# First expert slots of a two-layer MoE: another order for the ranks' chain, the hidden layer's low halves and `w2` on VectorE, earlier turning of the next rows, later weight loads

## The chip, the cores and the metric

The kernel runs on one core of a Trainium2 chip. The metric is device time in microseconds (us). The engines are TensorE (PE in the profile; PEld is its weight load), VectorE (DVE), ScalarE (ACT), GpSimd (POOL) and SyncE (SP), which here only issues DMAs. Each engine works through its own instructions in program order; a wait of one instruction holds everything behind it on that engine.

## The reference

Attention without softmax (a decaying state per head), then two mixture-of-experts layers. Each row goes to one of 8 experts, the one with the largest logit.

```
state = gamma * state + k[t] (outer) v[t];  y[t] = scale * q[t] @ state      # 4 x 8 heads, 768 steps, 64 wide
x = y as 3072 rows of 512
layer 1: e = argmax(x @ w_gate + bias[modality]); g = softmax(..)[e]
         x[row] = g * (relu(x[row] @ w1[e]) @ w2[e])                         # w1[e] 512x1024, w2[e] 1024x512
layer 2: e = argmax(x @ w_gate); g = softmax(..)[e]; o = sigmoid(x @ w_output_gate)[e]
         out[row] = g * o * (relu(x[row] @ w1[e]) @ w2[e])
```

## The kernel before

The attention is a loop of 24 units (line 772, `i` from 0 to 23). Its results are scattered to `x1d` in DRAM, each row at the place of its expert. Then each layer runs over slots of 256 rows, one expert each; which expert a slot has is known only on the chip. A slot fetches its rows into `xqb` (`xqf` in layer 1's first slot), turns them with DVE transposes into `xTb`, splits them into `xh` (ACT) and `xl` (DVE), multiplies by `w1` into `hT` (mm1, 96 matmuls of 256 columns), takes the ReLU as `hh` (ACT, line 960) and `hl` (DVE, line 961), multiplies by `w2` into `po` (mm2, 48 matmuls of 512 columns), and scales the result into `ob` (`done`, DVE, lines 1014 and 1017), which GpSimd scatters. Every product is made in three passes of reduced-precision numbers, high by high, high by low, low by high. So a loaded weight `raw` is split into a high half (`w1h`, `w2h`, ACT) and a low half (`w1l`, `w2l`, DVE, lines 514 and 521; one instruction of `w2l` covers a quarter of `w2`).

The first slot of each layer (`first`, line 1285; `first2` for layer 2) also has the end of the routing in it. The last rows of the layer before are transposed on PE (line 1051), their logits made (`lgm`, `lgs`), an expert chosen (`choose`, lines 185 to 212), ranks counted on PE (lines 218 and 220), and then DVE works out places: `total` (line 226 on), `place`, `weigh`, and `rp.blocks()`, which ends with line 368. This is called the ranks' chain here. Only then can the last rows be scattered, and the rows of the second slot be fetched (`s1.fetch`: half of them on SP's queue, half on ACT's). `rp.slots` (lines 378 to 420) makes the table of all slots.

What stands where in a slot is written by hand: `run` (line 1124) calls `at(f)` ahead of every `f` of mm1 (f = 0 to 7, 12 matmuls each, in the groups 0 to 3, 4 and 5, 6 and 7), and ahead of each eighth of mm2 (8 + j). `FIRST_AT` names the positions of transposes, `lgm`, `lgs`, count and total, place (the chain), scatter, choose, the step between the two transposes, and decide. `FIRST_W2` says at which position each quarter of `w2` is split, "h" on ACT, "l" on DVE. In first slots mm2 goes through its eighths in the order 0, 4, 1, 5, 2, 6, 3, 7; an eighth is six matmuls, and the first four eighths use quarters 0 and 1 of `w2`. Within them come four of `hh` by `w2h`, two of `hl` 0 by `w2h` (twice, once for each half of the rows), then two of `hl` 1, two by `w2l` 0, two by `w2l` 1. At j = 7, behind `done(0)`, the second slot's rows are turned (`Slot.turn`: the DVE transpose and `xh`).

SP's queue takes its DMAs in program order: at the end of attention the loads of q, k and v for the coming units, the first slot's weights, and the first slot's rows.

Of the kernel before, what the change touches and what calls it, by code (L numbers as in the profile page):

```python
# [424 lines left out]
def retention_moe_moe_kernel(ctx: ExitStack, tc: tile.TileContext, q, k, v, mod, mb, wg, wg2, w1, w2, cst_d, out):  # L425
    nc = tc.nc
# [195 lines left out]
    with ExitStack() as actx:  # L622
# [149 lines left out]
        for i in range(n):  # L772
# [57 lines left out]
            if i == i0 + 1:  # L830
                e0 = nc.values_load(rp1.star[0:1, 0:1], engines=[ENG.SP], min_val=0, max_val=E - 1, skip_runtime_bounds_check_because=why)
            if i0 < i <= i0 + 2:
                load(raw1, w1, e0, ks=(2 * (i - i0 - 1), 2 * (i - i0 - 1) + 1))
            if i0 + 2 < i <= i0 + 4:
                load(raw2, w2, e0, ks=(2 * (i - i0 - 3), 2 * (i - i0 - 3) + 1))
            if i == n - 4:
                fetch_rows(x1d, first_row(rp1), 2, xqf, xmf, after=scattered[-4:] + blanks)
        g1, ids = group1(n - 2, n, misc)
        ids()


    with ExitStack() as mctx:
# [30 lines left out]
        class Slot:  # L873
# [84 lines left out]

            def relu(self, b):
                nc.scalar.activation(hh[b], hT[b], AF.Relu)  # L960
                nc.vector.scalar_tensor_tensor(hl[b], in0=hT[b], scalar=0.0, in1=hh[b], op0=ALU.max, op1=ALU.subtract)  # L961

            def mm1(self, fs, at):
# [5 lines left out]
                for i, (m, f, k) in enumerate(todo):  # L969
                    if i % (3 * KD) == 0:  # L970
                        at(fs[i // (3 * KD)])
                    a, b = ((w1h, xh), (w1h, xl), (w1l, xh))[m]
                    nc.tensor.matmul(hT[f // 2][:, (f % 2) * 2 * P:(f % 2 + 1) * 2 * P], lhsT=a[k][:, f * P:(f + 1) * P], rhs=b[:, k, :],  # L973
                                     start=(m == 0 and k == 0 and f % 2 == 0), stop=(m == 2 and k == KD - 1), skip_group_check=True)
# [149 lines left out]
            def run(self, steps=(), nxt=()):  # L1124
# [3 lines left out]
                if not first:  # L1128
# [3 lines left out]
                    else:  # L1132
                        self.split2((0, 1))

                def group(f):
                    at(f)
                    if f == 5:
                        self.prepare()
                    if first:
                        for ks, parts in FIRST_W2[self.li - 1].get(f, ()):  # L1140
                            split2(ks, parts)

                for fs in ((0, 1, 2, 3), (4, 5), (6, 7)):
                    self.mm1(fs, group)
                    for f in fs[1::2]:
                        self.relu(f // 2)
                        if two and f % 4 == 3:
# [5 lines left out]
                for j, i in enumerate((0, 4, 1, 5, 2, 6, 3, 7) if first else range(8)):  # L1153
                    if first or j != 1:
                        group(8 + j)
                    if first and j == 5:
                        self.regs()
                        self.load(raw1, w1)
                        self.load(raw2, w2)
                    if first and j == 6:  # L1160
                        self.split1(0)
                    if j == (7 if first else 1):
                        if not first:
                            self.split1(0, "h")
                        self.coming(nxt, Slot.turn)
                        if not first:
                            group(9)
# [26 lines left out]
            def run_small(self, steps=(), nxt=()):  # L1194
# [21 lines left out]
                for j in range(4):  # L1216
# [29 lines left out]

        BIG_AT, SMALL_AT, FIRST_AT = (4, 7, 8, 15, 16, 16, 9, 1, 3), (1, 2, 4, 8, 8, 8, 5, 0, 2), (3, 4, 5, 6, 6, 8, 5, 0, 3)
        FIRST_W2 = [{3: [((0,), "hl")], 4: [((1,), "hl")], 6: [((2, 3), "h")], 8: [((2, 3), "l")]},
                    {f: [((f - 5,), "hl")] for f in range(5, 9)}]

# [34 lines left out]
        def first(li, steps, g, a, scatter):  # L1285
# [5 lines left out]
            def go(k):  # L1291
                if not rest:
                    rest.append(turns(g["place"](), g["weigh"](), rp.blocks()))
                for _ in zip(range(k), rest[0]):
                    pass
            s.run(steps + [(a, [lambda: go(100)]), (a + 1, [scatter]), (a + 2, [lambda: s1.fetch(after=before(), halves=(1,)), rp.slots]),
                           (max(9, a + 3), [lambda: s1.fetch(after=before(), halves=(0,), queue=nc.scalar)])], [s1])

# [11 lines left out]
        def first2(pend):  # L1310
            g, steps = pend.route(FIRST_AT, banks=[xT, hT[3]])
            run(rp2.order())
            first(2, steps[:7], g, FIRST_AT[4], pend.scatter)
# [83 lines left out]
```

## Time and profile before

| | |
|---|---|
| three runs | 792.72, 795.04 (median), 797.77 us |
| the profiled execution | 793.22 us, of which 791.4 us are its span |
| PE busy | 769.9 us, 97% of the span |
| DVE, ACT, POOL busy | 439.1, 282.4, 179.5 us |
| mean granted clock of PE | 0.999 |

The first slot of layer 1 runs on PE from 131 to 156 us, that of layer 2 from 462 to 489 us. Times of instructions are counted from the start of the span. A row of the timeline has the start and the length of a run of like instructions, and, in brackets, the idle time of the engine just before it with what ended that. Matmuls overlap, so the steps between the starts of rows tell what one costs.

### The profile page before, as it was taken

To read this page: it belongs to the slowest core of one execution; us is meant where nothing else is said; L and a number is where in the kernel's file an instruction comes from. 1 tells how busy PE (TensorE), PEld (TensorE's weight loads), DVE (VectorE), ACT (ScalarE), POOL (GpSimd) and SP (SyncE) were. 2 spreads that over 40 slices of the span, in tenths; PEclk is the share of its full clock that TensorE was granted. 3 is DMA by queue.
4 is the path that set the end of the run, shared out by engine and by line. 5 is a ranking of instruction groups with operands and counts; after the bars stand their busy time and mean duration, and the time that the engine had idled before them with its cause. 6 is when DMAs were issued, how large, how long until landed. Compare 5 with 4: busy or idle time off the path is not lost. (4 is left out here: it accounts for less than half of the span.)

```text
span 791.4 us, 18969 instructions
## 1 busy us (share of the span) xinstructions
PE 769.9 (97%) x6123; PEld 670.2 (85%) x6123; DVE 439.1 (55%) x1151; ACT 282.4 (36%) x507; POOL 179.5 (23%) x285
## 2 busy tenths in 40 slices
PE   8999999999999999999999988999999999999996
PEld 7888888788888978988899777888889888899785
DVE  4655488724344438334445887244656486473872
ACT  2444455312212234121212542124353563533641
POOL 4456653301110111110011112011302122011121
PEclk9999999999999999999999999999999999999999
DMA  9989899582211116221132343512716377271621
GB/s 190 184 192 216 219 285 298 186 282 57 56 42 29 42 44 234 66 56 41 45 82 70 137 148 108 190 53 69 254 38 236 80 247 249 54 239 46 223 71 53
DMA packets 137408, 107.06 MB, mean 135 GB/s; under 512 B 70269, under 2 KB 113405, under 8 KB 137216
## 3 DMA queue, kind: packets, MB, share of 16 engines
q1 hardware_dynamic: 125712, 85.15, 40.0%
q0 software_dynamic: 6400, 18.98, 6.5%
q10 hardware_dynamic: 5104, 0.75, 0.7%
q8 instruction: 74, 1.21, 0.7%
q14 instruction: 118, 0.97, 0.4%
HBM read 167.64 MB, written 25.83 MB: 244 GB/s over the span
## 5 line engine op out<-in xcount | busy, mean ns | idle before, releaser
L960 ACT ACTIVATE hh<-hT 128x512 fp32r<-128x512 f32 x96 | 57.3, 597 | 251.0 <-PE hT L973 251.0
L961 DVE SCALAR_TENSOR_TENSOR hl<-hT,hh 128x512 fp32r<-128x512 f32 x96 | 65.0, 687 | 131.5 <-ACT hh L960 113.4
L995 PE MATMUL po<-w2h,hl 128*128 128x512 f32 x400 | 113.9, 399 | 1.4 <-DVE hl L961 0.8
L995 PE MATMUL po<-w2l,hh 128*128 128x512 f32 x400 | 110.3, 396 | 1.8 <-DVE ob L1238 1.3
L995 PE MATMUL po<-w2h,hh 128*128 128x512 f32 x400 | 110.9, 399 | 0.0
L973 PE MATMUL hT<-xl,w1h 128*128 128x256 f32 x768 | 107.8, 282 | 0.0
L973 PE MATMUL hT<-xh,w1h 128*128 128x256 f32 x768 | 103.9, 282 | 3.7 <-ACT xh L555 3.5
L973 PEld LDWEIGHTS hT<-xh,w1h 128*128 128x128 f32 x768 | 96.2, 188 | 8.0 <-ACT xh L555 5.3
L973 PE MATMUL hT<-xh,w1l 128*128 128x256 f32 x768 | 102.0, 280 | 0.0
L973 PEld LDWEIGHTS hT<-xl,w1h 128*128 128x128 f32 x768 | 96.5, 188 | 4.5 <-issue 4.5
L973 PEld LDWEIGHTS hT<-xh,w1l 128*128 128x128 f32 x768 | 95.0, 188 | 0.0
L995 PEld LDWEIGHTS po<-w2l,hh 128*128 128x128 f32 x400 | 74.8, 188 | 21.1 <-DVE ob L1238 1.7
L995 PEld LDWEIGHTS po<-w2h,hl 128*128 128x128 f32 x400 | 73.6, 188 | 19.0 <-DVE hl L961 1.5
L995 PEld LDWEIGHTS po<-w2h,hh 128*128 128x128 f32 x400 | 73.1, 188 | 16.7 <-ACTq L1034 1.0
L475 POOL DMA_INDIRECT x2d<-ob,r_idx x28 | 30.3, 1081 | 246.1 <-DVE ob L265 134.3
L1030 POOL DMA_INDIRECT out_dram<-ob,to x28 | 37.1, 1325 | 176.5 <-DVE ob L1017 108.0
L555 ACT ACTIVATE xh<-xTb 128x512 fp32r<-128x512 f32 x58 | 33.4, 623 | 89.3 <-DVE xTb L550 49.3
L521 DVE TENSOR_TENSOR w2l<-raw,w2h 128x1024 fp32r<-128x1024 f32 x44 | 52.1, 1221 | 8.6 <-ACT w2h L519 3.2
L514 DVE TENSOR_TENSOR w1l<-raw,w1h 128x512 fp32r<-128x512 f32 x88 | 54.9, 687 | 0.5 <-ACT w1h L512 0.5
L512 ACT ACTIVATE w1h<-raw 128x512 fp32r<-128x512 f32 (+1 forms) x84 | 48.0, 639 | 1.7 <-ACTq L1038 1.0
L550 DVE STREAM_TRANSPOSE xTb<-xqb 128x1024 f32<-128x1024 f32 x29 | 36.0, 1243 | 22.5 <-DMA xmb<-x1d 10.6
L557 DVE TENSOR_TENSOR xl<-xTb,xh 128x512 fp32r<-128x512 f32 x58 | 37.5, 687 | 13.0 <-ACT xh L555 13.0
(217 smaller groups left out, 971.6 us busy)
## 6 DMA issues: line engine op xcount, KB each, us to landing
raw<-in_w_dram SPq DMA_DIRECT2D x248, 512.0 KB
xqb<-x2d SPq DMA_DIRECT2D x124, 64.0 KB
xqb<-x1d SPq DMA_DIRECT2D x108, 64.0 KB
nq<-in_q_dram SPq DMA_DIRECT2D x48, 128.0 KB
nk<-in_k_dram SPq DMA_DIRECT2D x24, 256.0 KB
nv<-in_v_dram SPq DMA_DIRECT2D x24, 256.0 KB
x1d<-zrow SPq DMA_DIRECT2D x4, 516.0 KB
x2d<-zrow SPq DMA_DIRECT2D x4, 516.0 KB
```

The costliest lines, as they stand in the source:

```text
L475: return nc.gpsimd.indirect_dma_start(out=dst, out_offset=bass.IndirectOffsetOnAxis(ap=rp.idx[:, t:t + 1], axis=0), in_=row, in_offset=Non ...
L512: nc.scalar.activation(w1h[i][:, cols], raw1[i][:, cols], AF.Copy)
L514: los[i].tensor_tensor(w1l[i][:, cols], raw1[i][:, cols], w1h[i][:, cols], op=ALU.subtract)
L521: nc.vector.tensor_tensor(w2l[i], raw2[i], w2h[i], op=ALU.subtract)
L550: nc.vector.transpose(xT[:, ks].rearrange("p k (a i) -> p a k i", i=32), xq.rearrange("p a (k i) -> p a k i", k=KD)[:, :, ks])
L555: nc.scalar.activation(hi[:, k:k + 2, :], xT[:, k:k + 2, :], AF.Copy)
L557: nc.vector.tensor_tensor(lo[:, k:k + 2, :], xT[:, k:k + 2, :], hi[:, k:k + 2, :], op=ALU.subtract)
L960: nc.scalar.activation(hh[b], hT[b], AF.Relu)
L961: nc.vector.scalar_tensor_tensor(hl[b], in0=hT[b], scalar=0.0, in1=hh[b], op0=ALU.max, op1=ALU.subtract)
L973: nc.tensor.matmul(hT[f // 2][:, (f % 2) * 2 * P:(f % 2 + 1) * 2 * P], lhsT=a[k][:, f * P:(f + 1) * P], rhs=b[:, k, :], start=(m == 0 and ...
L995: nc.tensor.matmul(po[h], lhsT=x[b][:, o:o + P], rhs=w[f // 2][:, f % 2, :], start=(m == 0 and f == 0), stop=(m == 2 and f == KF - 1))
L1030: nc.gpsimd.indirect_dma_start(out=out, out_offset=bass.IndirectOffsetOnAxis(ap=to[:, t:t + 1], axis=0), in_=o[:, :DM], in_offset=None, bo ...
```

## The change

- At the end of attention, the second half of `w1` is loaded at `i = n - 4`, behind the last q, k and v (before: one unit sooner), and `w2` at the next two units, behind the rows of the first slot `xqf` (before: half of it ahead of them).
- `relu` can put `hl` off. In first slots `hl` 0, 1 and 2 come at position 6, in `group`, behind `at(6)`.
- `mm1` calls `at` at every half position too.
- `FIRST_AT` has other positions: in layer 2 the transposes stand after 30 matmuls of mm1 (before 36), the logits at 3 and 4, and choose, count, total and the chain between 5 and 5.5; the scatter at 6, fetch and slots' table at 7.
- `FIRST_W2`: layer 1's quarter 0 is split one position sooner on ACT, and the low half of quarter 1 comes at 6 (before 4). In layer 2 the low halves of the quarters come at 7, 8, 9, 9 (before 5, 6, 7, 8).
- The second slot's rows are turned at j = 6, ahead of the split of the next `w1` and of `done(0)`.
- `rp2.order()` moves from the start of layer 2's first slot to behind `choose`.

```diff
@@ attention's loop
-            if i0 < i <= i0 + 2:
-                load(raw1, w1, e0, ks=(2 * (i - i0 - 1), 2 * (i - i0 - 1) + 1))
-            if i0 + 2 < i <= i0 + 4:
-                load(raw2, w2, e0, ks=(2 * (i - i0 - 3), 2 * (i - i0 - 3) + 1))
+            if i in (i0 + 1, n - 4):
+                load(raw1, w1, e0, ks=(0, 1) if i == i0 + 1 else (2, 3))
             if i == n - 4:
                 fetch_rows(x1d, first_row(rp1), 2, xqf, xmf, after=scattered[-4:] + blanks)
+            if n - 4 < i < n - 1:
+                load(raw2, w2, e0, ks=(0, 1) if i == n - 3 else (2, 3))
@@ relu
+            def relu(self, b, later=None):
                 nc.scalar.activation(hh[b], hT[b], AF.Relu)
-                nc.vector.scalar_tensor_tensor(hl[b], in0=hT[b], scalar=0.0, in1=hh[b], op0=ALU.max, op1=ALU.subtract)
+                def low():
+                    nc.vector.scalar_tensor_tensor(hl[b], in0=hT[b], scalar=0.0, in1=hh[b], op0=ALU.max, op1=ALU.subtract)
+                if later is None:
+                    low()
+                else:
+                    later.append(low)
@@ mm1
-                    if i % (3 * KD) == 0:
-                        at(fs[i // (3 * KD)])
+                    if i % 6 == 0:
+                        at(fs[i // (3 * KD)] + i % (3 * KD) / (3 * KD))
@@ run
                     if first:
+                        if f == 6:
+                            for low in later:
+                                low()
                         for ks, parts in FIRST_W2[self.li - 1].get(f, ()):
                             split2(ks, parts)
-                        self.relu(f // 2)
+                        self.relu(f // 2, later if first and f < 6 else None)
                     if first and j == 6:
+                        self.coming(nxt, Slot.turn)
                         self.split1(0)
                     if j == (7 if first else 1):
                         if not first:
                             self.split1(0, "h")
-                        self.coming(nxt, Slot.turn)
-                        if not first:
+                            self.coming(nxt, Slot.turn)
                             group(9)
@@ tables
-FIRST_AT = (3, 4, 5, 6, 6, 8, 5, 0, 3)
-        FIRST_W2 = [{3: [((0,), "hl")], 4: [((1,), "hl")], 6: [((2, 3), "h")], 8: [((2, 3), "l")]},
-                    {f: [((f - 5,), "hl")] for f in range(5, 9)}]
+FIRST_AT = (2.5, 3, 4, 5.5, 5.5, 7, 4, 0, 3)
+        FIRST_W2 = [{2: [((0,), "h")], 3: [((0,), "l")], 4: [((1,), "h")], 6: [((2, 3), "h"), ((1,), "l")], 8: [((2, 3), "l")]},
+                    {5: [((0,), "h")], 6: [((1,), "h")], 7: [((2,), "h"), ((0,), "l")], 8: [((3,), "h"), ((1,), "l")], 9: [((2, 3), "l")]}]
@@ first
-            s.run(steps + [(a, [lambda: go(100)]), (a + 1, [scatter]), (a + 2, [lambda: s1.fetch(after=before(), halves=(1,)), rp.slots]),
-                           (max(9, a + 3), [lambda: s1.fetch(after=before(), halves=(0,), queue=nc.scalar)])], [s1])
+            s.run(steps + [(a, [lambda: go(100)]), (6, [scatter]), (7, [lambda: s1.fetch(after=before(), halves=(1,)), rp.slots]),
+                           (9, [lambda: s1.fetch(after=before(), halves=(0,), queue=nc.scalar)])], [s1])
@@ first2
-            run(rp2.order())
+            steps[4][1].append(lambda: run(rp2.order()))
```

How the change stands in the engines' programs, at three places. The first is VectorE in layer 1's first slot, from the choice (line 209) to the total (line 226), before:

```order
L209 TENSOR_TENSOR r_oh<-rq_643,rm_0_646 128x16
L521 TENSOR_TENSOR w2l_104<-raw_88,w2h_100 128x1024
L961 SCALAR_TENSOR_TENSOR hl<-hT_116,hh 128x512
L961 SCALAR_TENSOR_TENSOR hl<-hT_117,hh 128x512
L521 TENSOR_TENSOR w2l_105<-raw_89,w2h_101 128x1024
L226 TENSOR_TENSOR rR_730<-misc,r_base 128x24
```

In the change one quarter of `w2l` is left there, and the two `hl` and the next quarter come behind the chain's last instruction (line 368), ahead of the slots' table (line 378 on):

```order
L368 TENSOR_SCALAR r_meta<-sfo_2434 128x1
L963 SCALAR_TENSOR_TENSOR hl<-hT_116,hh 128x512
L963 SCALAR_TENSOR_TENSOR hl<-hT_117,hh 128x512
L963 SCALAR_TENSOR_TENSOR hl<-hT_118,hh 128x512
L521 TENSOR_TENSOR w2l_105<-raw_89,w2h_101 128x1024
L378 TENSOR_TENSOR sm_0_2422<-sm_0_2421,cst 128x24
```

So two `hl` and one `w2l` have moved past the chain. The second place is VectorE in layer 2's first slot, behind the chain's end, before (`w2l_104`, quarter 0, stands ahead of the chain there; `w2l_107` is quarter 3):

```order
L368 TENSOR_SCALAR r_meta<-sfo_2437 128x1
L521 TENSOR_TENSOR w2l_105<-raw_89,w2h_101 128x1024
L521 TENSOR_TENSOR w2l_106<-raw_90,w2h_102 128x1024
L961 SCALAR_TENSOR_TENSOR hl<-hT_119,hh 128x512
L378 TENSOR_TENSOR sm_0_2425<-sm_0_2424,cst 128x24
```

In the change three `hl` follow line 368, then the slots' table, and behind its last instruction (line 413) stand all four quarters of `w2l`, `hl` 3 and the turn of the next rows (line 550):

```order
L413 CAST r_meta<-sld_2504 128x1
L521 TENSOR_TENSOR w2l_104<-raw_88,w2h_100 128x1024
L963 SCALAR_TENSOR_TENSOR hl<-hT_119,hh 128x512
L521 TENSOR_TENSOR w2l_105<-raw_89,w2h_101 128x1024
L521 TENSOR_TENSOR w2l_106<-raw_90,w2h_102 128x1024
L521 TENSOR_TENSOR w2l_107<-raw_91,w2h_103 128x1024
L891 TENSOR_LOAD r_meta
L550 STREAM_TRANSPOSE xTb<-xqb 128x8x4x32
```

So every quarter of `w2l` has moved behind the slots' table. The third place is TensorE in the first group of layer 2's mm1, where the last rows of layer 1 are transposed for their logits, before:

```order
L973 MATMUL hT_116<-xh,w1l_99 128x256
L1051 MATMUL xT<-ident,ob_2286 128x128 x4
L1051 MATMUL hT_119<-ident,ob_2286 128x128 x4
L973 MATMUL hT_116<-xh,w1l_96 128x256
L973 MATMUL hT_116<-xh,w1l_97 128x256
```

And in the change, with the logits (`misc<-oT,wgp`) six matmuls of mm1 behind them:

```order
L980 MATMUL hT_117<-xl,w1h_93 128x256
L1058 MATMUL xT<-ident,ob_2286 128x128 x4
L1058 MATMUL hT_119<-ident,ob_2286 128x128 x4
L980 MATMUL hT_117<-xl,w1h_94 128x256
L980 MATMUL hT_117<-xl,w1h_95 128x256
L980 MATMUL hT_116<-xh,w1l_96 128x256
L980 MATMUL hT_116<-xh,w1l_97 128x256
L980 MATMUL hT_116<-xh,w1l_98 128x256
L980 MATMUL hT_116<-xh,w1l_99 128x256
L1064 MATMUL misc<-oT,wgp_75 32x256 x4
```

The two sets of transposes have moved ahead of six matmuls of mm1, and the logits are six matmuls nearer to them.

## Rows read from the trace of the kernel before

**Rows 1.** The page's first part: busy time, share of the span, instructions.
```profile
PE 769.9 (97%) x6123; PEld 670.2 (85%) x6123; DVE 439.1 (55%) x1151; ACT 282.4 (36%) x507; POOL 179.5 (23%) x285
```

**Rows 2.** All waits of PE, 95 to 165 us: total, times, longest (us).
```profile
PE hT L973 <- ACT xh L555: 1.6, 2, 1.3
PE hT L667 <- DVE P L689: 0.7, 1, 0.7
```

**Rows 3.** Timeline of PE, layer 1's first slots: start, length, instruction, [idle before <- releaser].
```profile
139.78 0.18 PE L218 MATMUL misc<-r_oh,cb 128*128 128x16 bf16 x1
...
144.19 1.09 PE L995 MATMUL po<-w2h,hh 128*128 128x512 f32 x4
145.12 0.63 PE L995 MATMUL po<-w2h,hl 128*128 128x512 f32 x2
...
156.87 1.38 PE L973 MATMUL hT<-xh,w1h 128*128 128x256 f32 x7 [1.31 <-ACT xh L555]
...
181.13 0.17 PE L218 MATMUL misc<-r_oh,cb 128*128 128x16 bf16 x1 [0.59 <-DVE r_oh L212]
```

**Rows 4.** Timeline of DVE, layer 1's first slot.
```profile
140.21 1.28 DVE L961 SCALAR_TENSOR_TENSOR hl<-hT,hh 128x512 fp32r<-128x512 f32 x2
141.41 1.22 DVE L521 TENSOR_TENSOR w2l<-raw,w2h 128x1024 fp32r<-128x1024 f32 x1
142.54 0.17 DVE L226 TENSOR_TENSOR rR<-misc,r_base 128x24 f32<-128x24 f32 x1
...
146.07 0.15 DVE L368 TENSOR_SCALAR r_meta<-sfo 128x1 int32<-128x1 int32 x1
...
154.86 1.24 DVE L550 STREAM_TRANSPOSE xTb<-xqb 128x1024 f32<-128x1024 f32 x1
```

**Rows 5.** Timeline of ACT, end of layer 1's first slot.
```profile
156.19 1.15 ACT L555 ACTIVATE xh<-xTb 128x512 fp32r<-128x512 f32 x2 [11.21 <-DVE xTb L550]
```

**Rows 6.** Timeline of PE, layer 2's first slot.
```profile
467.26 0.66 PE L1051 MATMUL xT<-ident,ob 128*128 128x128 f32 x4 [0.94 <-DVE w1l L514]
...
477.33 0.86 PE L995 MATMUL po<-w2h,hh 128*128 128x512 f32 x3
...
481.57 0.73 PE L995 MATMUL po<-w2l,hh 128*128 128x512 f32 x2 [0.34 <-DVE w2l L521]
...
491.19 2.02 PE L973 MATMUL hT<-xh,w1h 128*128 128x256 f32 x15 [1.87 <-ACT xh L555]
```

**Rows 7.** Timeline of DVE, layer 2's first slot.
```profile
476.48 0.17 DVE L226 TENSOR_TENSOR rR<-misc,r_base 128x24 f32<-128x24 f32 x1
...
480.19 0.15 DVE L368 TENSOR_SCALAR r_meta<-sfo 128x1 int32<-128x1 int32 x1
480.29 2.36 DVE L521 TENSOR_TENSOR w2l<-raw,w2h 128x1024 fp32r<-128x1024 f32 x2
...
483.17 0.18 DVE L378 TENSOR_TENSOR sm<-sm,cst 128x24 f32<-128x24 f32 x1
...
484.97 0.14 DVE L413 CAST r_meta<-sld 128x1 int32<-128x1 f32 x1
```

**Rows 8.** Timeline of SP's DMA queue, end of attention.
```profile
120.85 1.88 SPq L538 DMA_DIRECT2D xqf<-x1d  x4
...
129.55 3.50 SPq L461 DMA_DIRECT2D x1d<-zrow  x4
```

**Rows 9.** Busy time in two stretches: engine busy (count), granted clock, DMA share, GB/s.
```profile
120.00:140.00 20.00, 19.59 (x265) 17.43 (x262) 16.21 (x59) 10.84 (x22) 8.68 (x13) 1.00 1.04 313
...
460.00:480.00 20.00, 17.54 (x136) 15.67 (x137) 17.67 (x76) 9.72 (x17) 2.82 (x3) 1.00 0.43 140
```

**Rows 10.** Timeline of ACT, end of layer 2's first slot.
```profile
490.21 1.15 ACT L555 ACTIVATE xh<-xTb 128x512 fp32r<-128x512 f32 x2 [11.13 <-DVE xTb L550]
```

**Rows 11.** Timeline of PE around 446 us, another slot's start.
```profile
445.98 1.16 PE L981 MATMUL hT<-w1h,xh 128*128 128x512 f32 x4 [0.92 <-issue]
```

**Rows 12.** Timeline of DVE, layer 2's second slot.
```profile
503.65 1.29 DVE L961 SCALAR_TENSOR_TENSOR hl<-hT,hh 128x512 fp32r<-128x512 f32 x2 [10.50 <-ACT hh L960]
```

More of the change, by code (lines that the diff above doesn't have):

```diff
@@ L957, in load @@
                 load(raw, w[(self.li - 1) * E:], self.ld[1], cond=self.ld[0], ks=ks)
-            def relu(self, b):
+            def relu(self, b, later=None):
                 nc.scalar.activation(hh[b], hT[b], AF.Relu)
-                nc.vector.scalar_tensor_tensor(hl[b], in0=hT[b], scalar=0.0, in1=hh[b], op0=ALU.max, op1=ALU.subtract)
+                def low():
[4 more added lines that the diff above has]
+                    later.append(low)
             def mm1(self, fs, at):
@@ L1133, in run @@
                         self.split2((0, 1))
+                later = []
                 def group(f):
@@ L1245, in run_small @@
                 at(8)
-        BIG_AT, SMALL_AT, FIRST_AT = (4, 7, 8, 15, 16, 16, 9, 1, 3), (1, 2, 4, 8, 8, 8, 5, 0, 2), (3, 4, 5, 6, 6, 8, 5, 0, 3)
-        FIRST_W2 = [{3: [((0,), "hl")], 4: [((1,), "hl")], 6: [((2, 3), "h")], 8: [((2, 3), "l")]},
-                    {f: [((f - 5,), "hl")] for f in range(5, 9)}]
+        BIG_AT, SMALL_AT, FIRST_AT = (4, 7, 8, 15, 16, 16, 9, 1, 3), (1, 2, 4, 8, 8, 8, 5, 0, 2), (2.5, 3, 4, 5.5, 5.5, 7, 4, 0, 3)
+        FIRST_W2 = [{2: [((0,), "h")], 3: [((0,), "l")], 4: [((1,), "h")], 6: [((2, 3), "h"), ((1,), "l")], 8: [((2, 3), "l")]},
+                    {5: [((0,), "h")], 6: [((1,), "h")], 7: [((2,), "h"), ((0,), "l")], 8: [((3,), "h"), ((1,), "l")], 9: [((2, 3), "l")]}]
         def step(li, i, pend=None):
```

## The prediction

> **What bounds the kernel now.** I read the page first. TensorE (PE) is busy 97% of the span [rows 1], so the 791.4 us can only shrink by the 21 us in which PE stands idle, and a change that moves other engines' work is worth what it takes out of those gaps or puts into them. Next I read PE's waits around the end of attention. From 95 to 165 us there are three: two for ScalarE's `xh` and one for the decay `P`; none is for a q, k or v tile or for a weight [rows 2]. Then I read PE's timeline in the first slot of layer 1: its second product starts at 144.19, and the next slot begins with a wait of 1.31 us for `xh`; later, 0.59 us goes by before the counts of the next slot's routing [rows 3]. VectorE's (DVE's) timeline tells why the rows come late. The ranks' chain (from the total, line 226, to the slots' order, line 368) begins at 142.54, after two low halves `hl` and two of `w2l`; the rows of the next slot, asked for behind it, are turned only after `done(0)`, at 154.86 [rows 4]. `xh` follows at 156.19 [rows 5]. In layer 2's first slot the same pieces lie otherwise: PE waits for the transposes, once for `w2l` (0.34), and 1.87 at the end [rows 6]; DVE has its chain from 476.48 to 480.34, then two `w2l`, then `hl` 3, then the slots' table [rows 7].
>
> **Loads at the end of attention.** The edit changes when 2 MB of weights are asked for, not how many. As no wait there is for q, k or v, asking for weights later takes nothing from PE: I cost it at 0. What covers the later arrival is time: the last parts of `w2` are first split some 12 us after they can be asked for. If that cover is gone, the row fetch is what suffers, since it must land before `xh` and PE's start at 131.17. It was issued at 120.85 and had landed by 129.55, when the zero fill that waits for it went out [rows 8]. Two more half-megabyte loads now stand close behind it. At the 313 GB/s of that stretch [rows 9], 1.05 MB take 3.35 us, so 0 to +3.35 us; I take 0, since they are issued behind the fetch, not ahead of it.
>
> **Layer 1's first slot.** Two `hl` and one `w2l` leave the place ahead of the chain: 1.28 + 1.22 = 2.50 us [rows 4]. The total would then begin at 140.04; the counts that it reads are issued by PE at 139.78 [rows 3], in the same place as before, so nothing new holds it. The chain takes 146.22 - 142.54 = 3.68 us and ends near 143.7. Behind it `hl` 0, 1, 2 take 0.6 each, to 145.5, then `w2l` 1 to 146.7. PE's first use of `hl` 0 is at 145.12 [rows 3]; a 512-column matmul takes 0.93/4 = 0.233 us there. In the code `hl` 1 comes 12 matmuls into the second product (147.0), `w2l` 0 after 14 (147.5) and `w2l` 1 after 16 (147.9). All are ready, by 0.8 us at the least. The scatter, the row fetch and the slots' table move up by about 2.5 us. The rows had been there for a turn at 154.86 without a wait, so they are there by 152.4 now, and the turn stands ahead of `done(0)`. `xh`'s first half ends 1.33 + 0.6 us after the turn starts, at 154.4. The second product ends at 156.87 - 1.31 = 155.56: the wait goes, **-1.31**. The turn puts 1.24 us on DVE ahead of `done(0)`, which nobody on PE waits for there. The 0.59 us of the next slot hangs on rows fetched later in the same queue; earlier requests may remove all or none of it, so I take **-0.3**, with 0 and -0.59 as the bounds. That also covers the loads that follow.
>
> **Layer 2's first slot.** The transposes stand six mm1 matmuls sooner, but in both kernels they wait until 467.26 for results that DVE reaches at its own time [rows 6]. Six matmuls of 256 columns (half of 0.233 each) are then still to do: +0.70. Behind them 60 mm1 matmuls (7.0 us) and the routing's small ones (about 1.0) filled 8.76 us up to 477.33, so some 0.7 us of short waits for the logits and the choice are there to be saved by asking sooner. I take +0.45 (0 to +0.9), and the second product starts at 477.8. The counts now stand 30 mm1 matmuls ahead of that, at about 474.3, so the chain starts about 474.4 and, 3.86 us long [rows 7], ends at 478.3. `hl` 0 is ready at 478.95, while PE wants it 0.93 us into the product, 478.73: +0.2. With `hl` 1 and 2 behind it DVE is free at 480.2. Here the edited table puts `w2l` 0 behind the slots' table, which takes 485.11 - 483.17 = 1.94 us [rows 7]: to 482.1. `w2l` 0 (1.18) is ready at 483.3. PE wants it 14 matmuls in, at 481.3: **+2.0**. Two matmuls later PE wants `w2l` 1, which stands behind `hl` 3: 483.3 + 0.6 + 1.2 = 485.1, against 483.8: **+1.3**. `w2l` 2 and 3 are done at 487.5 and wanted after 490. The old wait of 0.34 goes. Together 0.45 + 0.2 + 2.0 + 1.3 - 0.34 = **+3.6** on PE's second product; the bounds are +2 (chain half done sooner) and +4.5.
>
> **The gap behind it.** The 1.87 us is put down to `xh`. In layer 1 the product began 0.68 us after `xh`'s first instruction started (156.87 and 156.19); here it took 0.98 (491.19 and 490.21) [rows 3, 5, 6, 10]. `xh` was ready 0.3 us before PE began, so something of PE's own ended last. PE also stood for 0.92 us at 445.98, at a jump to another piece of code, with nothing waited for [rows 11]. The page of the Trainium skill "Runtime: NRT & Kernel Launch", section "Instruction fetch mechanics", says that a taken branch to a page of code outside the window breaks the sequential fetch, and the engine stands until the code has come; by that rule the gap follows PE's own branch and earlier rows can't remove it. No row here names what PE does in it. With rows that are now about 2 us earlier and a product that ends 3.6 later, `xh` is certainly early; if it alone set the gap, up to 1.57 us would go, and if PE's own step sets it, nothing goes. The offset of 0.3 us is nearer to the second: **0** (from -1.87). It could also grow: DVE stood 10.50 us ahead of the first `hl` of the next slot, at 503.65, while the next weights were in flight [rows 12]; if PE's step falls into that stretch and takes twice as long, that is +1.9.
>
> **Sum.** -1.31 - 0.3 + 3.6 = +2.0 us. The profiled execution took 793.22, which lies 1.8 below the median of the three runs (795.04); on it the sum gives 795.2, on the median 797.0. I forecast the middle, 796.0.
>
> **Rivals.**
> *The gap goes with the rows.* If `xh` alone sets the 1.87 us: 796.0 - 1.6 = 794.4. For it speaks the label of the wait; against it the 0.3 us. Chance 0.2.
> *Layer 1 gives nothing.* If the row fetch is not asked for sooner, because the landing of the scattered rows holds it, the 1.6 us stay: 797.6. The earlier total speaks against it. Chance 0.1.
> *The table does not stall PE.* If in layer 2 the slots' table is shorter or waits elsewhere and `w2l` arrives in time, +3.6 falls to +0.5 and the time to 792.9. Against it stand the measured 1.94 and 1.18 us. Chance 0.1.
> *The row fetch is slowed by the loads behind it*: +3.35, so 799.4. Chance 0.06.
> *Slower: PE's clock falls.* Two waits of 2.0 and 1.3 us, two matmuls apart, are new. If PE drops to 1.2 GHz after them, the 32 matmuls that are left of the 48 take 32 x 0.233 = 7.5 us more: 803.5, slower by over 1%. It decides only if the drop lasts the whole rest. The granted clock stayed at 1.00, that is 2.4 GHz, in the stretch with 2.46 us of idle time [rows 9]. The Trainium skill, "TensorE: Matmul & The Clock Gate", Part 1, says that the clock follows recent activity and idleness lowers it; this trace shows no drop at gaps as long. Chance 0.04.
>
> **Chances and range.** My forecast has 0.5. A change under 1% (8 us) is about what a measurement of this kernel can't tell from none. All cases but the clock's lie inside 1%: faster 0.02, same 0.93, slower 0.05. The range goes from 791.5 (no stall and the gap gone, on a fast base) to 799.5 (the slowed fetch); the three runs before alone span 5 us.
>
> **What would show it.** In the new trace: no wait for `xh` at the start of layer 1's second slot, with the turn ahead of `done(0)`; DVE's total near 140 there. In layer 2: the slots' table ahead of the first `w2l`, and two waits of PE for `w2l` of about 2.0 and 1.3 us near 481 and 484. The start of the next slot shows whether the gap is still 1.9 us with `xh` done well before. I would be wrong if PE shows no `w2l` wait there, if attention's end shows a new wait for `xTf` or `xqf`, or if the granted clock falls.

## The result and the profile after

| kernel | median us (range, runs) | ratio to the kernel before on the same chip, 95% interval |
|---|---|---|
| before | 795.09 (792.72 to 797.77, 6) | |
| the change | 802.33 (799.59 to 803.99, 6) | 1.0087 [1.0071, 1.0103] |
| the change on a second chip | 798.76 (794.43 to 802.32, 10) | 1.0037 [1.0011, 1.0063] |

The change made the kernel slower, by 7.2 us on the first chip and 3.9 on the second: under 1%, but clear of the noise on both. 796.0 was forecast, 791.5 to 799.5 as the range; the first median lies above it, the second inside. The profiled execution took 802.49 us, its span is 800.6 (before 793.22 and 791.4), and its mean granted clock is 0.988 (before 0.999). The granted clock is that of PE as a share of 2.4 GHz: 0.50 is 1.2 GHz, and a value between is read here as a stretch with some of each. The page of the change, PE's line and the granted clock in 40 slices, shows where to look: before, the clock had nines throughout [rows 1 has PE's line of before].

```profile
PE 775.6 (97%) x6123; PEld 675.2 (84%) x6123; DVE 440.6 (55%) x1151; ACT 282.8 (35%) x507; POOL 182.3 (23%) x285
...
PEclk9999999999999999999999997899999999999999
```

PE is busy for 5.7 us more with the same number of matmuls: they took longer. The slices with 7 and 8 lie from 480 to 520 us, in layer 2's first and second slot. PE's timeline of the change, layer 1's second slot and layer 2's first (start, length, instruction, idle time before it with its releaser):

```profile
157.51 0.75 PE L980 MATMUL hT<-xh,w1h 128*128 128x256 f32 x5
...
466.61 0.66 PE L1058 MATMUL xT<-ident,ob 128*128 128x128 f32 x4 [1.65 <-DVE w1l L514]
...
478.63 1.10 PE L1002 MATMUL po<-w2h,hh 128*128 128x512 f32 x4
...
483.91 0.73 PE L1002 MATMUL po<-w2l,hh 128*128 128x512 f32 x2 [1.57 <-DVE w2l L521]
485.64 1.22 PE L1002 MATMUL po<-w2l,hh 128*128 128x512 f32 x2 [1.00 <-DVE w2l L521]
...
487.52 1.91 PE L1002 MATMUL po<-w2l,hh 128*128 128x512 f32 x4
489.22 1.91 PE L1002 MATMUL po<-w2h,hh 128*128 128x512 f32 x4
...
499.36 3.77 PE L980 MATMUL hT<-xh,w1h 128*128 128x256 f32 x16 [3.19 <-issue]
502.94 3.20 PE L980 MATMUL hT<-xl,w1h 128*128 128x256 f32 x16
```

Layer 1's second slot starts without the wait that stood there [rows 3]. In layer 2 the wait ahead of the transposes has grown from 0.94 to 1.65, two waits for `w2l` (1.57 and 1.00) stand where one of 0.34 was, and the gap ahead of the second slot is 3.19 instead of 1.87 [rows 6]. Behind the waits, four 512-column matmuls take 489.22 - 487.52 = 1.70 us, where they had taken 0.93 [rows 3], and behind the gap sixteen of 256 columns take 502.94 - 499.36 = 3.58. The stretches of the change by window (busy time of PE, PEld, DVE, ACT, POOL; then the granted clock, DMA share, GB/s) say why. The kernel before has 1.00 in each of them.

```profile
460.00:470.00 10.00, 7.58 (x57) 6.33 (x57) 8.58 (x27) 2.87 (x6) 0.57 (x1) 0.90 0.63 216
470.00:480.00 10.00, 9.97 (x80) 8.92 (x73) 6.75 (x49) 6.04 (x9) 3.20 (x4) 0.93 0.14 50
480.00:485.00 5.00, 3.08 (x12) 1.84 (x11) 4.93 (x23) 0.37 (x1) 2.22 (x5) 1.00 0.38 87
485.00:490.00 5.00, 4.36 (x10) 3.47 (x11) 4.01 (x4) 0.89 (x2) 0.00 (x0) 0.50 0.70 211
490.00:495.00 5.00, 5.00 (x19) 3.94 (x18) 0.19 (x1) 0.27 (x1) 0.00 (x0) 0.82 0.95 352
...
500.00:505.00 5.00, 5.00 (x25) 5.00 (x25) 0.00 (x0) 0.00 (x0) 0.97 (x1) 0.50 0.16 60
```

The granted clock is 0.50 (1.2 GHz) from 485 to 490 and from 500 to 505, and below 1.00 around 470. Each time PE had stood idle just before: 1.65 us ahead of the transposes, 1.57 and 1.00 for `w2l`, 3.19 at the slot's end.

Between PE's milestones (the start of the first matmul of each stage in the timeline) the two profiled executions divide so:

| stage, us | before | change | difference |
|---|---|---|---|
| start to layer 2's first mm1 | 461.83 | 461.18 | -0.65 |
| layer 2's first slot, mm1 | 15.50 | 17.45 | +1.95 |
| its second product and the gap | 13.86 | 20.73 | +6.87 |
| second slot's mm1 | 11.30 | 14.07 | +2.77 |
| second slot's second product | 12.71 | 11.20 | -1.51 |
| from there to the last matmul | 269.13 | 268.92 | -0.21 |

Together +9.22. Of the third line, 2.57 - 0.34 = 2.23 are the `w2l` waits, 3.19 - 1.87 = 1.32 the gap, and 0.2 a short wait for `hl` 0 (the first four matmuls take 479.75 - 478.63 = 1.12 instead of 0.93); the 3.1 that are left are matmuls at the lower clock. The fourth line is all clock (16 matmuls in 3.58 us instead of 1.9). Of the second, an execution of the change whose clock stayed at 1.00 there needs 16.05 us (experiment 5), so 0.55 are its own and 1.4 the clock's. That makes about 7.3 us of clock, and 1.9 us net of everything else.

This is one pair of executions, and both are far out. The profile of before, at 0.999, shows less of the low clock than most of its executions: 31 of them on the second chip have 0.993 to 0.998, 0.9965 on the mean. In the change's profile on the second chip the four lines of layer 2 come to +6.45 us instead of +10.08, and by the same division 3.2 of these are the clock's.

VectorE's timeline of the change shows both parts at work. In layer 1 the total begins at 142.16, the turn stands ahead of `done(0)` (line 1021), and DVE then waits 1.22 us for PE to finish that half's product:

```profile
142.16 0.18 DVE L226 TENSOR_TENSOR rR<-misc,r_base 128x24 f32<-128x24 f32 x1 [0.45 <-PE misc L220]
...
145.71 0.15 DVE L368 TENSOR_SCALAR r_meta<-sfo 128x1 int32<-128x1 int32 x1
...
153.85 1.24 DVE L550 STREAM_TRANSPOSE xTb<-xqb 128x1024 f32<-128x1024 f32 x1
156.31 0.75 DVE L1021 TENSOR_SCALAR ob<-po,xmf 128x512 f32<-128x512 f32 x1 [1.22 <-PE po L1002]
```

In layer 2 the first `w2l` comes only behind the slots' table, at 482.64:

```profile
478.94 0.15 DVE L368 TENSOR_SCALAR r_meta<-sfo 128x1 int32<-128x1 int32 x1
479.01 1.88 DVE L963 SCALAR_TENSOR_TENSOR hl<-hT,hh 128x512 fp32r<-128x512 f32 x3
480.80 0.17 DVE L378 TENSOR_TENSOR sm<-sm,cst 128x24 f32<-128x24 f32 x1
...
482.58 0.14 DVE L413 CAST r_meta<-sld 128x1 int32<-128x1 f32 x1
482.64 1.21 DVE L521 TENSOR_TENSOR w2l<-raw,w2h 128x1024 fp32r<-128x1024 f32 x1
483.77 0.68 DVE L963 SCALAR_TENSOR_TENSOR hl<-hT,hh 128x512 fp32r<-128x512 f32 x1
484.37 3.49 DVE L521 TENSOR_TENSOR w2l<-raw,w2h 128x1024 fp32r<-128x1024 f32 x3
```

The next rows' `xh` on ScalarE, and the next expert's weights on SP's queue, in the change:

```profile
489.11 1.15 ACT L555 ACTIVATE xh<-xTb 128x512 fp32r<-128x512 f32 x2 [8.74 <-DVEq L1041]
```

```profile
485.77 5.71 SPq L506 DMA_DIRECT2D raw<-in_w_dram  x8
```

`xh` is done at 490.3, 9 us ahead of the slot that needs it. The gap of 3.19 has nothing to do with the rows.

### The profile page after: what moved, and what is told of

Its sections match the earlier page's. It is cut to its first block, busy times and chain, and to the rows that moved or that the text cites. A ratio compares the mean times of both kernels' runs of the same rounds, so it can differ in the third digit from the quotient of the medians.

```text
span 800.6 us, 18964 instructions
## 1 busy us (share of the span) xinstructions
PE 775.6 (97%) x6123; PEld 675.2 (84%) x6123; DVE 440.6 (55%) x1151; ACT 282.8 (35%) x507; POOL 182.3 (23%) x285
## 5 line engine op out<-in xcount | busy, mean ns | idle before, releaser
L1037 POOL DMA_INDIRECT out_dram<-ob,to x28 | 40.5, 1447 | 189.6 <-DVE ob L1024 113.0
L519 ACT ACTIVATE w2h<-raw 128x1024 fp32r<-128x1024 f32 x44 | 44.4, 1049 | 0.7 <-PE po L1002 0.6
```

Of the source, the lines that this page charges most:

```text
L519: nc.scalar.activation(w2h[i], raw2[i], AF.Copy)
L1037: nc.gpsimd.indirect_dma_start(out=out, out_offset=bass.IndirectOffsetOnAxis(ap=to[:, t:t + 1], axis=0), in_=o[:, :DM], in_offset=None, bo ...
```

## The experiments

Theory A is that PE's new waits in layer 2's first slot let the clock fall and that the clock is the larger part of the loss; theory B that the waits cost their own length only. Theory J is on the gap: it is PE's own step to the next piece of code, lengthened by the weights in flight. All ratios are to the kernel before on the same chip.

**1. The slots' table behind the first `w2l`.**

```diff
-7: [((2,), "h"), ((0,), "l")], 8: [((3,), "h"), ((1,), "l")]
+7: [((2,), "h"), ((0, 1), "l")], 8: [((3,), "h")]
-(7, [lambda: s1.fetch(after=before(), halves=(1,)), rp.slots])
+(7, [lambda: s1.fetch(after=before(), halves=(1,))]), (7 if li == 1 else 8, [rp.slots])
```

> The change with one thing else: in layer 2's first slot the low halves of w2's quarters 0 and 1 stand ahead of the slots' table on DVE, the table behind them. Theory A (the two waits for w2l let PE's clock fall, and the clock is the larger part of the loss): the waits fall from 2.57 us to about 0.4, the stretch from 485 to 492 us runs at a granted clock of 1.00, and the kernel takes 5 to 6 us less than the change (about 797). Theory B (the waits cost their own length, the clock falls for another reason): 2.2 us less (about 800), with the clock still at 0.5 behind the second product's first part.

795.64 us, 1.0008 [0.9993, 1.0022]. Waits and clock of this kernel, PE's timeline and the window:

```profile
482.51 0.73 PE L1002 MATMUL po<-w2l,hh 128*128 128x512 f32 x2 [0.39 <-DVE w2l L521]
...
494.73 3.51 PE L980 MATMUL hT<-xh,w1h 128*128 128x256 f32 x16 [4.49 <-issue]
```

```profile
480.00:490.00 10.00, 9.61 (x42) 7.22 (x40) 9.36 (x27) 1.15 (x2) 1.98 (x4) 1.00 0.53 149
```

The wait fell to 0.39 and the clock stayed at 1.00 through the second product. By the ratios the change is 0.9 or 0.4% above before, and this kernel 0.1%: 6.3 us less than the change by its first result, 2.3 by its second. On this chip experiment 4, the change but for its loads, took 798.02: 2.4 us more, close to the 2.2 that theory B forecast. So the times don't decide between A and B. The profile does: the slow matmuls of the second product (3.1 us in the change's first profile) went with 2.2 us of waits. The gap did not shrink; it is 4.49 (2.88 in experiment 4), and the clock fell behind it.

**2. The kernel before with such a wait put in.** The table right behind the chain in layer 2, ahead of three quarters of `w2l`:

```diff
-(a, [lambda: go(100)]), (a + 1, [scatter]), (a + 2, [lambda: s1.fetch(after=before(), halves=(1,)), rp.slots])
+(a, [lambda: go(100)] + ([rp.slots] if li == 2 else [])), (a + 1, [scatter]),
+(a + 2, [lambda: s1.fetch(after=before(), halves=(1,))] + ([rp.slots] if li == 1 else []))
```

> The kernel before with one thing else: in layer 2's first slot the slots' table (1.94 us on DVE) stands right behind the chain, so ahead of w2l of quarter 1, 2 and 3. PE then waits about 2.2 us for w2l, near 481.5 us, where it waited 0.34. Theory A: the granted clock falls to 0.5 behind that wait and the kernel takes 4 to 6 us more than before (799 to 801). Theory B: 1.9 us more (797), the clock stays at 1.00.

796.44 us, 1.0029 [1.0011, 1.0047], its runs from 794.99 to 800.28. PE's wait and the clock behind it:

```profile
482.53 0.85 PE L995 MATMUL po<-w2l,hh 128*128 128x512 f32 x2 [2.13 <-DVE w2l L521]
```

```profile
480.00:485.00 5.00, 2.87 (x9) 1.93 (x8) 4.93 (x17) 0.00 (x0) 3.13 (x4) 0.80 0.32 72
485.00:490.00 5.00, 5.00 (x20) 4.00 (x19) 0.35 (x1) 0.00 (x0) 0.59 (x2) 0.86 0.78 232
```

In the kernel before these two stretches had 1.00. So one wait of 2.13 us, in a kernel that is otherwise the old one, was followed by the lower clock: that such a wait can bring it down is shown. The size was missed, 1.6 us by the medians and 2.3 by the ratio, instead of theory A's 4 to 6; theory B's 1.9 was nearer. From the second product's start to the second slot it lost 17.95 - 13.86 = 4.1 us: 1.8 of longer wait, 0.8 of longer gap (2.66) and 1.5 of clock. But 1.5 of these came back in the second slot (22.51 us to the third slot's first matmul, before 24.01): PE was late enough there for VectorE's `hl`, for which it had waited before. And some runs hardly lost at all.

**3. Layer 2's own part as before.** `FIRST_AT`, layer 2's `FIRST_W2`, `hl` put off in layer 1 alone, `rp2.order()` at the start; loads, layer 1 and turn as in the change.

```diff
-FIRST_AT = (2.5, 3, 4, 5.5, 5.5, 7, 4, 0, 3)
+FIRST_AT = (3, 4, 5, 6, 6, 8, 5, 0, 3)
-later if first and f < 6 else None
+later if first and f < 6 and self.li == 1 else None
-(6, [scatter]), (7, [lambda: s1.fetch(after=before(), halves=(1,)), rp.slots])
+(a + 1, [scatter]), (a + 2, [lambda: s1.fetch(after=before(), halves=(1,)), rp.slots])
```

> The change with all of layer 2's own part as before (positions, w2's splits, hl not put off, order at the start); the loads, layer 1's part and the earlier turn stay. If the whole loss arises in layer 2's first slot: no low clock there, and 0.5 to 2 us below before (793 to 794.5). If the loads or layer 1's part lose as well: at or above 796.

792.52 us, 0.9978 [0.9964, 0.9992]: faster than the kernel before, by 0.2%. The whole loss arises with layer 2's own part, in its first slot. The low clock is not gone, as was expected; it stands behind the gap, which is 2.29 here:

```profile
490.00:495.00 5.00, 5.00 (x32) 5.00 (x31) 0.60 (x1) 0.00 (x0) 0.56 (x1) 0.67 0.94 317
```

It costs little: the second slot takes 512.95 - 488.80 = 24.15 us to the third slot's first matmul, before 24.01, since the wait for `hl` that stood there is gone.

**4. Loads at the end of attention as before**, the rest as in the change (the diff's first hunk undone).

> The change with w1's and w2's loads at the end of attention as before. PE stood 0.89 and 0.98 us with nothing seen to wait for at the end of attention in the change and reached layer 1's first product 2.2 us later than before. If the later loads cause that: about 2 us less than the change (800) and no such gaps there. If not: same as the change (802.3, within 1).

798.02 us, 1.0037 [1.0016, 1.0059], the same ratio as the change on the second chip. On the first chip the change is slower still, so this alone left it open. The two gaps are not there, but layer 1 began later still, at 134.94. VectorE's turn of the first slot's rows waits for their fetch, and PE for `xh`, where before it waited 0.31:

```profile
133.52 1.30 DVE L550 STREAM_TRANSPOSE xTf<-xqf 128x512 f32<-128x512 f32 x2 [1.14 <-DMA xqf<-x1d]
```

```profile
134.94 2.13 PE L980 MATMUL hT<-xh,w1h 128*128 128x256 f32 x16 [1.44 <-ACT xh L555]
```

With the old loads `xqf` stands in SP's queue behind half of `w2`: it was asked for at 123.96 here, in the change at 118.02.

**5. The change once more**, on another chip, for its time against its clock.

> The change itself once more, as the base of this chip and to see how its time and its mean granted clock go together from run to run. If the time that differs is the clock's: the runs with the lower mean clock are the longer ones, by about 0.8 us for each 0.001. Median 799 to 803.

798.76 us, 1.0037 [1.0011, 1.0063]. Its ten runs by mean granted clock: 794.43 at 0.998; 797.88, 796.2 at 0.996; 795.39 at 0.995; 798.06 at 0.994; 799.45, 799.58, 800.73 at 0.992; 802.32 at 0.988; 802.02 at 0.986. A line through them falls 0.67 us for each 0.001 of clock, so the time goes with the clock as expected; the median lies just below the expected 799. The one run whose clock held (0.998) took 794.43, the median of before on this chip is 794.90. The mean clock of the ten is 0.993, that of before 0.9965: by that line 2.4 of the 3.9 us, an estimate. In this profile the clock was 1.00 from 460 to 475 in spite of a wait of 1.67 ahead of the transposes, and mm1 took 477.49 - 461.44 = 16.05 us: the same wait brings the clock down in one execution and not in another.

**6. The next expert's `w2` asked for late**, when PE has begun the second product's last matmul; otherwise the change.

```diff
 self.load(raw1, w1)
-self.load(raw2, w2)
+if self.li == 1:
+    self.load(raw2, w2)
...
+if first and self.li == 2:
+    self.load(raw2, w2, after=[self.last.ins])
```

> The change with one thing else: in layer 2's first slot the next expert's w2 (half of the 4 MB) is asked for only when PE has begun the last matmul of the second product. Theory J (the gap ahead of layer 2's second slot is PE's own step to the next piece of code, lengthened by the weights in flight): the gap falls from 3.2 to 2 us or less, and the slow clock behind it goes or shrinks; 1 to 4 us less than the change in all. Rival (the gap has a length of its own, whatever is in flight): the gap stays at 3 us, and the time too.

796.36 us, 1.0023 [1.0006, 1.0041]. PE's timeline:

```profile
494.29 2.13 PE L982 MATMUL hT<-xh,w1h 128*128 128x256 f32 x16 [1.39 <-DVEq L1043]
```

The gap is 1.39, and the sixteen matmuls behind it are at full pace (2.13 us to the end of the last one, where the change had 3.77). The stretch inside the gap, here and then in the change (the last two figures are the DMA share and GB/s):

```profile
492.90:494.20 1.30, 0.00 (x1) 0.00 (x0) 1.07 (x2) 0.00 (x0) 1.08 (x1) 1.00 0.14 24
```

```profile
496.20:499.30 3.10, 0.00 (x0) 0.00 (x0) 1.31 (x2) 0.00 (x0) 1.32 (x1) 0.90 1.03 384
```

`xh` was early in both, and the one edit is when `w2` is asked for. Theory J holds in this profile, and the rival, a gap of fixed length, falls. The waits ahead of the gap were those of the change (1.67, 1.56 and 1.00), and the clock fell behind them as there, to 0.66 from 465 to 470 and to 0.84 and 0.82 between 480 and 490. On the same chip the change took 798.76, 2.4 us more.

**7. Experiment 3 with the turn behind `done(0)` again.**

```diff
 if first and j == 6:
-    self.coming(nxt, Slot.turn)
     self.split1(0)
 if j == (7 if first else 1):
     if not first:
         self.split1(0, "h")
-        self.coming(nxt, Slot.turn)
+    self.coming(nxt, Slot.turn)
```

> Layer 2's own part as before, as in the third experiment, and also the turn of the next rows behind done(0) again. If the earlier turn carries the gain in layer 1: PE waits 1.0 to 1.4 us for xh ahead of layer 1's second slot and the kernel is 1.0 to 1.5 us above the third experiment (793.5 to 794). If the earlier chain carries it: no such wait, and 792.5. In layer 2 the gap ahead of the second slot stays within 0.5 us of the third experiment's 2.3 by theory J.

793.89 us, 0.9992 [0.9976, 1.0009]. VectorE and PE at the start of layer 1's second slot:

```profile
153.49 0.75 DVE L1021 TENSOR_SCALAR ob<-po,xmf 128x512 f32<-128x512 f32 x1 [2.34 <-PE po L1002]
154.15 1.23 DVE L550 STREAM_TRANSPOSE xTb<-xqb 128x1024 f32<-128x1024 f32 x1
```

```profile
156.16 2.43 PE L980 MATMUL hT<-xh,w1h 128*128 128x256 f32 x16 [1.32 <-ACT xh L555]
```

The wait is back, 1.32, with the chain as early as in the change: the turn queues behind `done(0)`, which waits 2.34 us for PE.

**8. Experiment 3 with the late `w2` of experiment 6.**

> The third experiment (layer 2's own part as before, the rest of the change kept) with the late w2 of the second experiment of this call. If the gap is lengthened by the weights in flight: the gap falls from 2.3 to 1.5 to 2 us, the granted clock stays at 1.00 from 485 to 500, and 0.5 to 2 us less than the third experiment: 790.5 to 792. If not: 792.5.

792.55 us, 0.997 [0.9956, 0.9983]. The gap is 2.30, that of experiment 3 is 2.29: nothing gained, and the clock behind it is 0.67 from 490 to 495 as there. The edit hardly moved `w2`: the second product ends earlier in this kernel, and SP issued the eight loads in 6.58 us, in experiment 3 in 6.79 (in experiment 6 in 13.19). So this is no test of theory J.

**9. Transposes after 36 matmuls again**, the rest as in the change.

```diff
-FIRST_AT = (2.5, 3, 4, 5.5, 5.5, 7, 4, 0, 3)
+FIRST_AT = (3, 3.5, 4, 5.5, 5.5, 7, 4, 0, 3)
```

> The change with one thing else: in layer 2's first slot the two sets of transposes stand after 36 matmuls of mm1 again (before the change 36, in it 30), the logits after 42. The wait for w1l ahead of the transposes falls from 1.65 to 0.94 us, and the step from layer 2's first matmul to its second product from 16.1 to 17.5 us to 15.5 to 16. If that wait is what lets the clock fall at 466 to 471 us in some executions: no low clock there in the profile, and 0.5 to 2 us less than the change on one chip (about 797 to 798, where the change had 798.8). The w2l waits and what follows from them stay.

796.75 us, 1.0021 [1.0001, 1.0041]. The wait is 0.94 again:

```profile
465.19 0.66 PE L1058 MATMUL xT<-ident,ob 128*128 128x128 f32 x4 [0.94 <-DVE w1l L514]
```

mm1 takes 475.13 - 459.76 = 15.37 us, less than before (15.50), and the clock is 1.00 from 460 to 475. By the ratio it is 0.2% below the change on the second chip, but the two intervals overlap.

**10. Experiments 1 and 9 together.**

> Both mends together: transposes after 36 matmuls, and w2l of quarters 0 and 1 ahead of the slots' table. What is left of the loss is then the gap ahead of layer 2's second slot. If the two waits and the clock behind them are the whole loss: as the third experiment, 792.5 to 794, and below the kernel before. If layer 2's other new positions cost too: 795 or more.

793.91 us, 0.9986 [0.9974, 0.9998]. With the two waits mended the loss is gone, 2.8 us less than experiment 9 on the same chip. The gap is still 3.65, and the clock is 0.73 from 490 to 495 behind it.

**11. The kernel before with the earlier turn alone** (the hunk of experiment 7, the other way round).

> The kernel before with the earlier turn alone (next rows turned at j = 6, ahead of done(0), in both first slots). The rows of layer 1's second slot had landed only shortly ahead of their turn, so if the turn needs the earlier chain to pay: the wait for xh in layer 1 stays at 0.8 to 1.3 us, and 794.5 to 795. If the turn alone carries the gain: the wait goes, and 793.5.

794.33 us, 0.999 [0.997, 1.001]. VectorE's turn and PE in layer 1:

```profile
155.06 1.25 DVE L550 STREAM_TRANSPOSE xTb<-xqb 128x1024 f32<-128x1024 f32 x1 [2.33 <-DMA xmb<-x1d]
```

```profile
157.65 1.55 PE L973 MATMUL hT<-xh,w1h 128*128 128x256 f32 x11 [1.27 <-ACTq L1034]
```

Without the earlier chain the turn stands there and waits 2.33 us for the rows, and PE waits 1.27. So the gain in layer 1 needs both, the chain and the turn; experiment 7 shows one missing, this one the other.

**12. Experiment 3 with the old loads**: of the change, layer 1's part and the turn alone.

> The third experiment (layer 2's own part as before) with the loads at the end of attention as before too, so that of the change only layer 1's part and the earlier turn are left. If the later loads cost or gain nothing: 792.5, within 0.7 of the third experiment. If they cost: 791 or less; if they gain: 794 or more. The step from layer 1's first matmul to its second slot stays 1.5 us shorter than in the kernel before.

794.21 us, 0.9969 [0.995, 0.9988]. The time is 1.7 above experiment 3, of which 0.9 is the chip's by the medians of before (795.72 here, 794.82 there); the ratio is that of experiments 3 and 8 within the intervals. So the times show no cost of the later loads and don't settle a gain. The profile has one: as in experiment 4, the turn of `xqf` waits for its fetch (0.81) and PE waits 1.11 for `xh` ahead of layer 1. That is so in two of the five profiles with the old loads and in none of the nine with the later ones. This is also the best that came out of the study: layer 1's part with layer 2 left alone, 0.2 to 0.3% below the kernel before.

## Why the prediction was wrong

**Loads, 0.** Not contradicted by the times: the ratios of experiments 3 and 12 agree with and without them. The rival had the sign wrong: `xqf` was not delayed by them but asked for 2.8 us sooner (118.02 instead of 120.85), and the old order made PE wait for it in experiments 4 and 12. The profile of the change has two short "issue" gaps of PE at 130 and 133 us, and reached layer 1 2.2 us later than before. The eight other profiles with the same code there were at 130.56 to 133.29, none with such gaps, against 131.17 before. I leave what the gaps were open.

**Layer 1, -1.3 and -0.3.** Right, and somewhat more. From the second product to the second slot PE needs 11.20 us instead of 12.68, in every kernel that has chain and turn; the 0.59 us for the next slot's counts is gone too. The mechanism was as told: neither part alone does it. The total began at 142.16 in a profile in which layer 1 started 2.2 later, so 140.0 in the prediction's count, where 140.04 stood.

**Layer 2, mm1, +0.45.** The wait ahead of the transposes grew by 0.71, as worked out (0.70), and the stage by 0.55 where the clock held. What I did not see is that a wait of 1.65 can bring the clock down, +1.4 in this profile. It did so in three of the five profiles that have this wait (the change, experiments 4 and 6) and not in two (experiments 1 and 5).

**The waits for `w2l`, 2.0 and 1.3.** They are there, in the place and order forecast, 1.57 and 1.00: a fifth to a quarter shorter, 2.57 instead of 3.3. The first low half was ready 483.85 - 478.63 = 5.2 us into the product instead of 5.5. The +0.2 for `hl` 0 came as 0.2.

**The gap, 0.** The reading that PE's own step sets it was right: `xh` was done 9 us early and the gap stayed. Its size was wrong in a direction that I had only as a bound, +1.9: it grew by 1.3 in the first profile of the change and 1.8 in the second. The earlier chain and slots' table also bring the next expert's weights forward (485.77 instead of 488.09), and PE, late by its waits, steps to the next code when all of them have been asked for. The runs fall into two groups by that (PE's gap and SP's issue of the weights, from the timelines; the time between has the gap in it):

| kernel | weights issued | second slot starts | between, us | gap, us |
|---|---|---|---|---|
| 6, `w2` late | 483.83, `w2` held back | 494.29 | | 1.39 |
| before | 488.09 | 491.19 | 3.1 | 1.87 |
| 11 | 488.42 | 491.67 | 3.3 | 2.08 |
| 7 | 486.64 | 490.12 | 3.5 | 1.95 |
| 12 | 487.31 | 490.97 | 3.7 | 2.06 |
| 8 | 485.46 | 489.23 | 3.8 | 2.30 |
| 3 | 484.75 | 488.80 | 4.1 | 2.29 |
| 10 | 482.84 | 490.97 | 8.1 | 3.65 |
| 2 | 485.99 | 494.46 | 8.5 | 2.66 |
| 1 | 485.76 | 494.73 | 9.0 | 4.49 |
| 4 | 487.84 | 499.91 | 12.1 | 2.88 |
| 9 | 482.06 | 494.48 | 12.4 | 3.14 |
| change, second chip | 484.28 | 497.21 | 12.9 | 3.68 |
| change | 485.77 | 499.36 | 13.6 | 3.19 |

With the weights out for 4 us or less the gap is 1.9 to 2.3; with them out for 8 to 14 us it is 2.7 to 4.5, without growing further with the time. Only experiment 6 changes the traffic alone; the other rows agree with it but differ in more. The Trainium skill, "Runtime: NRT & Kernel Launch", section "Instruction fetch mechanics", says that after a taken branch to code outside the window an engine waits for the fetch of that code. The runs agree in that the gap follows the traffic (1.39 us at 24 GB/s, 3.19 at 384) and not the rows, but none of these rows shows the fetch itself.

**Left out of the sum:** the second slot's `hl` wait [rows 12 has VectorE's side of it]. A PE that comes late, or runs at the lower clock behind the gap, no longer waits there: -1.5 in the change. In experiments 3, 8, 11 and 12 the clock fell behind the gap too (0.67 to 0.73 from 490 to 495), and the second slot took 24.1 us against 24.0 before, because the slow matmuls took the place of this wait.

**The step that failed** is the last rival, "Slower: PE's clock falls", with a chance of 0.04. Its mechanism is what happened. I turned it down because a stretch with 2.46 us of idle time had stood at 1.00 [rows 9], and asked that the drop last the whole rest of the product to matter. Both were wrong. The 2.46 us were a sum of shorter waits; the longest of them is this one, and the longest of the whole kernel is 1.87 [rows 6]:

```profile
461.17 0.73 PE L995 MATMUL po<-w2l,hh 128*128 128x512 f32 x2 [1.29 <-DVE ob L1238]
```

That was no proof for the 2.0 and 1.3 that the prediction put close together, let alone for 3.19; the trace of before had no gap as long. And the clock need not stay down: it fell behind three idle times in a row, for a part of mm1, of the second product and of the next slot's mm1, 1.4, 3.1 and 2.8 us. The sum put these 7.3 us at nothing. Without the clock it gave +2.0, and +1.9 was measured without it, but that is luck in part: the gap's +1.3, the missing `hl` wait's -1.5, the late start of layer 1 and what the rest of layer 1 gained are not in the sum and nearly cancel. The clock made +9.2 out of +1.9. The page "TensorE: Matmul & The Clock Gate" of the Trainium skill, Part 1, has the rule that speaks for this (the clock follows recent activity, and idleness lowers it), and I let one row of before outweigh it. The runs agree where it fell, but not every idle time brought it down (last section).

What stays open: the change lost 0.9% on one chip and 0.4% on another. Runs at a clock of 0.994 took 799.6 and 802.2 us on the first and 798.1 on the second, so it is not the mean clock alone. What decides whether a given idle time is followed by the lower clock is open too.

## What to carry to other kernels

On a kernel in which PE is 97% busy, price a new wait of PE like these as a spread and not a number: its own length, and the matmuls behind it at half the clock in some executions. Here 1.8 us of new wait cost 1.6 to 2.3 us (experiment 2); the change, with 4.3 us of new idle time in three places, lost 9.2 us in one profile and 3.9 by the medians of another chip. A single profile of before can have more luck with the clock than most of its runs. Moving work on VectorE behind a chain pays only if PE doesn't want that work before the chain's end: the same exchange, with the earlier turn, was worth 1.5 us in layer 1, where `w2l` was ready over 1 us ahead of its use, and cost 2.2 us more of waits in layer 2, where it was not. When one change touches two stages, take them apart: layer 1's part of this one, alone, is faster than the kernel that it started from.

## What the runs showed of the hardware that I had not expected

- In the change, waits of PE of 1.65 and of 1.57 and 1.00 us and a gap of 3.19 were followed by a granted clock of 0.79, 0.50 and 0.50 over 5 us; gaps of 1.87 and 1.31 in the kernel before by 1.00. The length alone doesn't tell. The same wait of 1.65 to 1.67 was followed by 0.79 and 0.66 over 5 us in the change and in experiments 4 and 6, and by 1.00 in experiments 1 and 5. Gaps of 2.06 to 2.30 were followed by 0.67 to 0.73 (experiments 3, 8, 11, 12), one of 2.66 by 1.00 (experiment 2).
- So one kernel on one chip took from 794.4 (mean clock 0.998) to 802.3 us (0.988).
- PE's step from one piece of code to the next took as little as 1.39 us of its time with 2 MB of the next weights held back and hardly any DMA traffic, and up to 4.49 with all 4 MB asked for, with nothing on the page to wait for ("issue", or a queue's line).
